# The third and fourth unit's weight scale within the first product, and VectorE work held behind a layer output's maximum

## The chip, the cores and the metric

The kernel runs on one core of a Trainium2 chip. TensorE (PE) multiplies, VectorE (DVE), ScalarE (ACT) and GpSimd (POOL) do the elementwise work, and SyncE (SP) issues DMAs. The metric is the device time of one execution in microseconds.

## The reference

Attention over 4 batches, 8 heads, 576 positions and 64 columns, whose softmax keeps only scores within `tau` = 0.02 of the row's maximum; then two feed-forward layers over the 2304 tokens, 512 to 2048 to 512 columns, all in f32:

```python
scores = scale * q @ k.T
scores = where(scores >= max(scores) - tau, scores, -1e9)
x = softmax(scores) @ v            # as (2304, 512)
h = x @ w_in;   x = (h * clip(h + 3, 0, 6) / 6) @ w_out      # layer 1
h = x @ w_in2;  out = (max(h, 0) ** 2) @ w_out2              # layer 2
```

## The kernel before, in words

**Precision.** Each f32 operand of a layer is split into an f16 high part and an f16 residue, scaled by a power of two, and a product is three f16 matmuls: high by high, residue by high, high by residue. The scales need maxima: of each group of weights, and of each layer's input.

**Blocks.** A batch of 576 tokens is one block. Layers and batches alternate: layer 1 of batch 0, layer 2 of batch 0, layer 1 of batch 1, and so on, eight blocks. A block takes 16 blocks of 128 hidden columns in four quarters. `hidden(f)` makes one of them: 24 matmuls into the PSUM tile `hp` (L685), then relu on ScalarE, `g` on VectorE (L690 or L693), the high part `gh` (L695, ScalarE) and the residue `gl` (L696, GpSimd). `output(qd)` multiplies a quarter with the output weights, four tiles `y` (L722), which VectorE adds to `ya` (L728) from the second quarter on.

**Borders.** Behind the last quarter of a layer 1, the block's output must be scaled for layer 2. For each of the four tiles there is an absolute maximum (L730); their maximum `gm` (L733) goes through a matmul `vm` (L119) which brings it to all partitions, then `mx` (L121), `ex` (L126) and the scale `sx` (L737). By it ScalarE (L386) and VectorE (L387) write the halves of the next layer's input, with which its first `hp` begins. The text calls the four passages from a layer 1 to its layer 2 the first to fourth border.

**Weights.** They come in units of 256 hidden columns, 1 MB each: 32 units, in the first two blocks alone (later blocks load the split weights back from DRAM). The order is `wseq`: two units of input weights, two more, two of output weights, and so on; so the third and fourth unit are input weights of the second quarter, and the fifth holds the first output weights. `group_scale` takes the scale of two units at once: an absolute maximum of each (L544, VectorE), `gm` (L546), again `vm` (L119), `mx` (L121), `sp` (L126, L550) and a few numbers of 128x1. `w_next` makes the halves: ScalarE scales (L611), VectorE shifts and merges bits (L614 and L615 for the first four units; for the others ScalarE's L619 and VectorE's merge L620), ScalarE writes the high part (L622), GpSimd the residue (L623), and SyncE stores both. There are 4 load buffers; a unit's buffer is free behind its merge.

**Order.** The program is written as generators: each step of a block asks `tick` for the weights that are due (`EARLY` gives the step at which the third to eighth unit are due, `LEAD` that of all later ones), and after each step the main loop hands out a share of the attention of the next batch (`attn_to`): scores, the softmax in two parts, the transposes of the probabilities by DMA, and five tiles later the product with v. A scheduler then sets the order in which each engine issues. `tc.issue_after(i)` gives it an edge: what is traced inside it on the engine of `i` is issued behind `i`. The tiles `s`, `hp` and `y` share three PSUM buffers; `vm`, the transposes and attention's product share two others.

## Time and profile before

| | |
|---|---|
| median of 3 runs | 1097.5 us (1095.11 to 1100.58) |
| profiled execution, its time | 1097.44 us |
| its span, first to last instruction | 1095.7 us |
| mean granted TensorE clock | 0.967 |
| TensorE busy | 1014.6 us (93%) |
| ScalarE busy | 654.4 us (60%) |
| VectorE busy | 642.9 us (59%) |
| GpSimd busy | 502.0 us (46%) |

Busy time is that of instructions that compute, weight loads aside; an engine that waits in its queue is idle. Of the 81 us in which TensorE isn't busy, most lies in the first 400 us, where attention of the first batches and the making of the weights go on beside the layers. A row's bracket tells how long the engine stood idle before it, and what released it.

### The profile page before, as it was taken

Reading aid. Unit: us, or ns where it says so; the run is one execution under the profiler, and the core shown is the slowest. Engines: PE = TensorE matmul, PEld = TensorE weight load, DVE = VectorE, ACT = ScalarE, POOL = GpSimd, SP = SyncE. Lnnn points to the kernel's source line nnn. Section 1 sums busy time; section 2 is a strip of 40 time slices with the busy share of each in tenths; the row PEclk is TensorE's granted clock in tenths of the full one; section 3 lists DMA queues with packets and bytes.
Section 4 is the critical chain, followed back from the end, with each engine's and each line's share of the span. In section 5 each row is a group of like instructions: output and inputs, shape, how many; then the busy total and the mean of one; then the engine's idle time right before and its main releaser. Section 6 shows DMA issues by size and latency. Waiting matters only on the chain.

```text
span 1095.7 us, 23283 instructions
## 1 busy us (share of the span) xinstructions
PE 1014.6 (93%) x9248; PEld 819.2 (75%) x9248; DVE 642.9 (59%) x1344; ACT 654.4 (60%) x1128; POOL 502.0 (46%) x629
## 2 busy tenths in 40 slices
PE   6877698897987999999999999999999999998998
PEld 4655476676776888888788888888788887776776
DVE  6885789889778875455855554555834231233122
ACT  5896798877887875655675555655654243313222
POOL 5886656755656754344355334443444222212111
PEclk9999799898988999999999999999999999999999
DMA  9999689896877686656565555555464342222211
GB/s 271 186 181 234 197 313 289 253 215 175 198 190 213 144 200 168 146 119 150 127 139 125 141 143 140 132 130 133 94 139 116 105 121 83 92 77 78 78 39 44
DMA packets 258748, 167.58 MB, mean 153 GB/s; under 512 B 215888, under 2 KB 228176, under 8 KB 258640
## 3 DMA queue, kind: packets, MB, share of 16 engines
q1 hardware_dynamic: 257072, 165.71, 60.3%
q8 instruction: 72, 1.18, 0.4%
q10 hardware_dynamic: 1568, 0.39, 0.2%
q14 instruction: 36, 0.29, 0.1%
HBM read 98.57 MB, written 21.50 MB: 110 GB/s over the span
## 4 chain that ended last, share of the span: by engine, by line
PE 72%; DVE 13%; DMA 7%; ACT 5%; issue 2%; POOL 1%; ACTq 0%; POOLq 0%; DVEq 0%
PE hp L685 30%; PE y L722 30%; PE s L295 4%; PE o L350 4%; DMA pt<-p 2%; DVE nm L301 2%; DVE wc L620 2%; DMA wd<-in_moe_w_out_dram 1%; DVE e L318 1%; DMA vraw<-in_v_dram 1%; PE s L291 1%; DVE ya L728 1%; PE tps L180 1%; DMA pt<-wpo 1%; DMA wd<-in_moe_w_in_dram 1%
## 5 line engine op out<-in xcount | busy, mean ns | idle before, releaser
L685 PE MATMUL hp<-x,wpi 128*128 128x288 f16 x3072 | 405.7, 291 | 13.8 <-ACT wpi L622 5.2
L685 PEld LDWEIGHTS <-wpi 128*128 128x128 f16 x3072 | 300.1, 99 | 94.7 <-ACT wpi L622 5.5
L722 PEld LDWEIGHTS <-wpo 128*128 128x128 f16 x3072 | 297.5, 99 | 92.7 <-DVE e L318 7.9
L722 PE MATMUL y<-gh,wpo 128*128 128x288 f16 x2048 | 338.7, 288 | 15.9 <-DVE e L318 7.5
L696 POOL TENSOR_TENSOR gl<-g,gh 128x576 f16<-128x576 f32 x128 | 168.6, 1318 | 299.6 <-ACT gh L695 298.9
L722 PE MATMUL y<-gl,wpo 128*128 128x288 f16 x1024 | 209.2, 288 | 0.0
L301 DVE TENSOR_REDUCE nm<-s 128x1 f32<-128x576 f32 x144 | 107.6, 750 | 58.7 <-PE s L295 55.3
L728 DVE SCALAR_TENSOR_TENSOR ya<-y,yq,ya 128x576 f32<-128x576 f32 (+1 forms) x97 | 77.9, 809 | 97.5 <-PE y L722 97.3
L326 POOL TENSOR_TENSOR p<-e,p 128x512 f16<-128x512 f32 x108 | 127.2, 1178 | 0.0
L695 ACT ACTIVATE gh<-g 128x576 f16<-128x576 f32 x128 | 86.9, 680 | 56.0 <-DVE g L693 27.9
L318 DVE SCALAR_TENSOR_TENSOR e<-s,thr,e 128x576 f32<-128x576 f32 x108 | 87.9, 814 | 38.9 <-ACT e L311 38.0
L324 ACT ACTIVATE p<-e 128x576 f16<-128x576 f32 x108 | 73.5, 681 | 51.3 <-DVE e L318 41.1
L350 PE MATMUL o<-v,pt 128*128 128x64 f16 (+1 forms) x2016 | 90.5, 200 | 12.2 <-ACT os L357 4.0
L350 PEld LDWEIGHTS <-pt 128*128 128x128 f16 x2016 | 80.6, 101 | 24.1 <-issue 9.3
L295 PE MATMUL s<-k_st,q_st 128*128 128x288 f32 x480 | 94.5, 320 | 0.6 <-DVE g L690 0.3
L693 DVE TENSOR_TENSOR g<-g,hp 128x576 f32<-128x576 f32 x64 | 48.0, 750 | 64.6 <-ACT g L692 64.4
L690 DVE SCALAR_TENSOR_TENSOR g<-g,r_w,hp 128x576 f32<-128x576 f32 x64 | 51.9, 810 | 57.8 <-ACT g L689 57.7
L689 ACT ACTIVATE g<-hp,r_h,aq 128x576 f32<-128x576 f32 x64 | 52.9, 829 | 53.7 <-PE hp L685 52.9
L692 ACT ACTIVATE g<-hp,r_w 128x576 f32<-128x576 f32 x64 | 47.1, 736 | 57.1 <-PE hp L685 55.9
L311 ACT ACTIVATE e<-s,nm 128x576 f32<-128x576 f32 x108 | 78.5, 727 | 0.4
L325 POOL TENSOR_TENSOR p<-e,p 128x64 f16<-128x64 f32 x108 | 35.2, 326 | 95.0 <-issue 59.2
L333 POOL TENSOR_SCALAR sm<-sm,vsc 128x2 f32<-128x2 f32 (+1 forms) x80 | 23.0, 287 | 112.7 <-DVE e L318 99.7
(127 smaller groups left out, 1138.5 us busy)
## 6 DMA issues: line engine op xcount, KB each, us to landing
wpi<-scr SPq DMA_DIRECT2D x48, 512.0 KB, 3.7
wpo<-scr SPq DMA_DIRECT2D x48, 512.0 KB, 4.1
wd<-in_moe_w_in_dram SPq DMA_DIRECT2D x16, 1024.0 KB, 7.2
wd<-in_moe_w_out_dram SPq DMA_DIRECT2D x16, 1024.0 KB, 6.9
scr<-wpi SPq DMA_DIRECT2D x16, 512.0 KB, 6.9
scr<-wpo SPq DMA_DIRECT2D x16, 512.0 KB, 5.0
kraw<-in_k_dram SPq DMA_DIRECT2D x16, 256.0 KB, 4.3
vraw<-in_v_dram SPq DMA_DIRECT2D x16, 256.0 KB, 3.2
```

Of the source, the lines that this page charges most:

```text
L295: nc.tensor.matmul(s[:, half, 0:HALF], lhsT=u.qs[sl][:, cs], rhs=u.ks[sl][:, kk, c], start=i == 0, stop=i == len(ops) - 1)
L301: nc.vector.tensor_reduce(out=j.nm, in_=j.s, axis=AX.XY, op=ALU.min)
L311: nc.scalar.activation(out=j.e, in_=j.s, func=AF.Exp, bias=j.nm, scale=-1.0)
L318: nc.vector.scalar_tensor_tensor(out=j.e, in0=j.s, scalar=j.thr, in1=j.e, op0=ALU.is_le, op1=ALU.mult, accum_out=u.sm[:, col:col + 1])
L324: nc.scalar.activation(out=p16[:, 0:S], in_=e, func=AF.Copy)
L326: nc.gpsimd.tensor_tensor(out=p16[:, S + TAIL:], in0=e[:, 0:NT * P], in1=p16[:, 0:NT * P], op=ALU.subtract)
L350: nc.tensor.matmul(o[:, n * w:n * w + w], lhsT=j.pt[:, c, :], rhs=vv[:, hs, vc, :], start=i == 0, stop=i == len(ops) - 1)
L685: last_hp[0] = nc.tensor.matmul(hp[:, a, 0:HALF], lhsT=wsl(tag, "i", f, w, c), rhs=x[c][:, a * HALF:(a + 1) * HALF], start=i == 0, stop=i ...
L695: nc.scalar.activation(out=gh, in_=gf, func=AF.Copy)
L696: nc.gpsimd.tensor_tensor(out=gl, in0=gf, in1=gh, op=ALU.subtract)
L722: nc.tensor.matmul(a[:, k_, 0:HALF], lhsT=wsl(tag, "o", f, w, e), rhs=g[f][:, k_ * HALF:(k_ + 1) * HALF], start=i == 0, stop=i == len(ops) ...
L728: nc.vector.scalar_tensor_tensor(out=y, in0=av_, scalar=yq, in1=y, op0=ALU.mult, op1=ALU.add)
```

## The change

There are three edits. The third and fourth unit's scale (`group_scale`) was called where the third unit was made, in an edge behind the last matmul of the step before (`last_hp`); now it is called within the first `hp`, behind its third chunk of input columns of four. `EARLY` makes the third to eighth unit due one or two steps sooner. And `border` remembers the instruction of the layer 1 output's `gm`; from there to the fourth step of layer 2, weights and attention are traced in an edge behind it, so that their VectorE instructions are issued behind `gm`.

```diff
@@ -26,7 +26,7 @@
 FIRST_LD = 34
 FIRST_ATT = 15
 PRE = 6
-EARLY = {2: 3, 3: 3, 4: 4, 5: 5, 6: 6, 7: 8}
+EARLY = {2: 1, 3: 1, 4: 2, 5: 3, 6: 5, 7: 7}
 SPLIT = 34
 FIRST_DVE = 4
 N_G, N_PT = 3, 7
@@ -572,8 +572,6 @@
                 nc.vector.tensor_scalar(out=e_y[L][:, c], in0=a_w[L][:, c], scalar1=e_w[L][:, c], scalar2=eo, op0=ALU.mult, op1=ALU.mult)
         return sp
 
-    last_hp = [None]
-
     def norm_scale(q):
 
         n = NQ // UC
@@ -602,9 +600,6 @@
             return
         while n_ld[0] <= k:
             w_load()
-        if k == len(FIRST_W):
-            with tc.issue_after(last_hp[0].ins):
-                group_scale(k)
         sp = group_scale(k)
         d = w_raw.pop(k)
         c = t = wt.tile([P, UW], F32, name="wc", bufs=3)
@@ -637,12 +632,18 @@
         while n_sp[0] <= k:
             w_next()
 
+    border = [None]
+
+    def behind():
+        return tc.issue_after(border[0].ins) if border[0] is not None else nullcontext()
+
     def tick(step):
         while n_sp[0] < len(wseq):
             k = n_sp[0]
             if EARLY.get(k, UC * k - LEAD) > step:
                 break
-            w_next()
+            with behind():
+                w_next()
 
     def wsl(tag, kind, f, part, j):
         w = w_hl[wuse[(tag, kind, f // UC)]]
@@ -682,8 +683,11 @@
             for c in range(NC):
                 for w, x in ((0, xh), (1, xh), (0, xl)):
                     for a in range(2):
-                        last_hp[0] = nc.tensor.matmul(hp[:, a, 0:HALF], lhsT=wsl(tag, "i", f, w, c), rhs=x[c][:, a * HALF:(a + 1) * HALF], start=i == 0, stop=i == 3 * NC - 1)
+                        mm = nc.tensor.matmul(hp[:, a, 0:HALF], lhsT=wsl(tag, "i", f, w, c), rhs=x[c][:, a * HALF:(a + 1) * HALF], start=i == 0, stop=i == 3 * NC - 1)
                     i += 1
+                if gstep[0] == 1 and c == NC - 2:
+                    with tc.issue_after(mm.ins):
+                        group_scale(n_sp[0])
             g = me.tile([P, 2, HALF], F32, name="g", bufs=N_G)
             if layer == 1:
                 nc.scalar.activation(out=g, in_=hv, func=AF.Relu, bias=r_h[:, q:q + 1], scale=aq[q])
@@ -730,9 +734,10 @@
                     nc.vector.tensor_reduce(out=y4[:, e:e + 1], in_=ya[:, e, :], axis=AX.X, op=ALU.max, apply_absolute_value=True)
                     if e == NC - 1:
                         am = st.tile([P, 1], F32, name="gm", bufs=2)
-                        nc.vector.tensor_reduce(out=am, in_=y4, axis=AX.X, op=ALU.max)
+                        gm = nc.vector.tensor_reduce(out=am, in_=y4, axis=AX.X, op=ALU.max)
                         s2 = st.tile([P, 1], F32, name="sx", bufs=2)
                         xsc["e"] = st.tile([P, 1], F32, name="ex", bufs=2)
+                        border[0] = gm
                         unit_of(xsc["e"], all_max(am, ident_s))
                         nc.vector.reciprocal(out=s2, in_=xsc["e"])
                         split_scaled([ya[:, c, :] for c in range(NC)], s2)
@@ -823,7 +828,10 @@
 
         for g, _ in enumerate(moe(tag, layer, b, xs)):
             if nxt is not None:
-                attn_to(min(nxt + LAG, start + math.ceil(todo * (g + 1) / ng)))
+                with behind():
+                    attn_to(min(nxt + LAG, start + math.ceil(todo * (g + 1) / ng)))
+            if layer == 2 and g == 3:
+                border[0] = None
 
 
 # ---- launch: one core; inputs and outputs as the reference has them ----
```

VectorE in the first product, from the last part of x on. `x` is the first layer's input, `k_st` keys of attention, the first `mx` to `r_h` belong to the scale of the weights, `wc` to the weights themselves. Before:

```order
L379 SCALAR_TENSOR_TENSOR x_1581<-xT,sx,x_1581 128x256
L220 TENSOR_TENSOR k_st_94<-tps,k_st_94 64x256
L220 TENSOR_TENSOR k_st_96<-tps,k_st_96 64x256
L121 TENSOR_REDUCE mx<-vm 128x1
L690 SCALAR_TENSOR_TENSOR g<-g,r_w_106,hp 128x576
L121 TENSOR_REDUCE mx<-vm 128x1
L126 TENSOR_SCALAR sp<-mx 128x1
L556 TENSOR_SCALAR e_w_102<-mx 128x1
L556 TENSOR_SCALAR a_w_104<-mx 128x1
L690 SCALAR_TENSOR_TENSOR g<-g,r_w_106,hp 128x576
L126 TENSOR_SCALAR sp<-mx 128x1
L550 RECIPROCAL sp<-sp 128x1
```

And now, from the same instruction on:

```order
L379 SCALAR_TENSOR_TENSOR x_1581<-xT,sx,x_1581 128x256
L121 TENSOR_REDUCE mx<-vm 128x1
L126 TENSOR_SCALAR sp<-mx 128x1
L556 TENSOR_SCALAR e_w_102<-mx 128x1
L556 TENSOR_SCALAR a_w_104<-mx 128x1
L550 RECIPROCAL sp<-sp 128x1
L563 RECIPROCAL rw<-a_w_104 128x1
L564 TENSOR_SCALAR r_w_106<-rw,e_w_102 128x1
L565 TENSOR_SCALAR r_h<-rw,e_w_102 128x1
L677 TENSOR_SCALAR aq_1888<-e_w_102,r_w_106 128x1
L678 TENSOR_TENSOR aq<-aq_1888,ex 128x1
L121 TENSOR_REDUCE mx<-vm 128x1
```

The scale of the third and fourth unit has moved ahead of the first `g`, and so have the numbers that follow from it and the next `mx`, that of the first output weights.

VectorE at the first border, from the maximum `gm` to the scale `sx`. `nm`, `e`, `sm` and `os` are attention's softmax, `am` and `vsc` the scale of v, `q_st` queries; `wc` and `g_4139` are weights. Before:

```order
L733 TENSOR_REDUCE gm<-y_3258 128x1
L546 TENSOR_REDUCE gm<-g_3794 128x1
L591 RECIPROCAL r_w_107<-mx 128x1
L592 TENSOR_SCALAR a_w_105<-mx,e_w_103 128x1
L318 SCALAR_TENSOR_TENSOR e,sm<-s,thr,e 128x576
L230 SCALAR_TENSOR_TENSOR q_st_90<-tps,qs,q_st_90 64x64
L334 RECIPROCAL sm<-sm 128x1
L712 MEMSET y_11125 128x1
L121 TENSOR_REDUCE mx<-vm 128x1
L126 TENSOR_SCALAR ex<-mx 128x1
L737 RECIPROCAL sx<-ex 128x1
```

And now, from `gm` on:

```order
L737 TENSOR_REDUCE gm<-y_3258 128x1
L589 RECIPROCAL r_w_107<-mx 128x1
L590 TENSOR_SCALAR a_w_105<-mx,e_w_103 128x1
L301 TENSOR_REDUCE nm<-s 128x1
L318 SCALAR_TENSOR_TENSOR e,sm<-s,thr,e 128x576
L243 TENSOR_REDUCE am<-vraw 128x1
L301 TENSOR_REDUCE nm<-s 128x1
L615 SCALAR_TENSOR_TENSOR wc<-wc,wd 128x1024
L546 TENSOR_REDUCE gm<-g_3794 128x1
L243 TENSOR_REDUCE am<-vraw 128x1
L716 MEMSET y_11125 128x1
L230 SCALAR_TENSOR_TENSOR q_st_90<-tps,qs,q_st_90 64x64
```

...and from there to `sx`, with nothing left out between:

```order
L121 TENSOR_REDUCE mx<-vm 128x1
L318 SCALAR_TENSOR_TENSOR e,sm<-s,thr,e 128x576
L544 TENSOR_REDUCE g_4139<-wd 128x1
L334 RECIPROCAL sm<-sm 128x2
L318 SCALAR_TENSOR_TENSOR e,sm<-s,thr,e 128x576
L126 TENSOR_SCALAR ex<-mx 128x1
L230 SCALAR_TENSOR_TENSOR q_st_92<-tps,qs,q_st_92 64x256
L361 TENSOR_TENSOR os<-o,sm 128x2x64
L334 RECIPROCAL sm<-sm 128x1
L742 RECIPROCAL sx<-ex 128x1
```

Nine instructions stood between `gm` and `sx`, one of them of 128x576; now there are twenty, and nine of these are of 128x576 or more.

VectorE at the second border, from `gm` to `sx`. Before:

```order
L733 TENSOR_REDUCE gm<-y_7556 128x1
L251 TENSOR_SCALAR vsc<-vsc 128x1
L318 SCALAR_TENSOR_TENSOR e,sm<-s,thr,e 128x576
L712 MEMSET y_13828 128x1
L252 RECIPROCAL vsc<-vsc 128x1
L318 SCALAR_TENSOR_TENSOR e,sm<-s,thr,e 128x576
L121 TENSOR_REDUCE mx<-vm 128x1
L253 TENSOR_SCALAR vsc<-vsc 128x1
L361 TENSOR_TENSOR os<-o,sm 128x2x64
L126 TENSOR_SCALAR ex<-mx 128x1
L737 RECIPROCAL sx<-ex 128x1
```

And now, where `gm`, one `nm`, one `e` and `vsc` stand ahead of these rows:

```order
L301 TENSOR_REDUCE nm<-s 128x1
L716 MEMSET y_13828 128x1
L121 TENSOR_REDUCE mx<-vm 128x1
L361 TENSOR_TENSOR os<-o,sm 128x2x64
L252 RECIPROCAL vsc<-vsc 128x1
L318 SCALAR_TENSOR_TENSOR e,sm<-s,thr,e 128x576
L334 RECIPROCAL sm<-sm 128x1
L301 TENSOR_REDUCE nm<-s 128x1
L126 TENSOR_SCALAR ex<-mx 128x1
L253 TENSOR_SCALAR vsc<-vsc 128x1
L361 TENSOR_TENSOR os<-o,sm 128x2x64
L742 RECIPROCAL sx<-ex 128x1
```

Fourteen instructions stand between `gm` and `sx` in place of nine, three `nm`, two `e` and two `os` among them.

## Rows read from the trace of the kernel before

**Rows 1.** Windows (A:B, length in us): each engine's busy us, clock, DMA, GB/s.

```profile
160.00:170.00 10.00, 6.96 (x43) 5.15 (x42) 9.94 (x22) 9.93 (x15) 6.14 (x7) 0.84 0.81 245
190.00:200.00 10.00, 7.96 (x44) 5.45 (x45) 9.61 (x25) 9.83 (x15) 3.53 (x6) 0.66 0.66 117
450.00:500.00 50.00, 50.00 (x491) 41.22 (x489) 28.46 (x58) 28.93 (x54) 22.90 (x29) 1.00 0.62 144
530.00:547.00 17.00, 14.56 (x167) 12.78 (x167) 15.79 (x46) 11.52 (x23) 6.21 (x9) 0.90 0.49 116
```

**Rows 2.** Timeline of TensorE, first stage: start us, us, instruction, [idle before <-releaser].

```profile
123.21 0.66 PE L685 MATMUL hp<-x,wpi 128*128 128x288 f16 x2 [5.17 <-ACT wpi L622]
...
128.35 1.14 PE L722 MATMUL y<-gh,wpo 128*128 128x288 f16 x4 [4.48 <-ACT wpo L622]
```

**Rows 3.** Timeline of VectorE, same stage, same columns.

```profile
110.06 0.48 DVE L379 SCALAR_TENSOR_TENSOR x<-xT,sx,x 128x256 f16<-128x256 f32 x1 [0.64 <-ACT x L378]
...
113.73 0.29 DVE L121 TENSOR_REDUCE mx<-vm 128x1 f32<-128x128 f32 x1 [1.77 <-PE vm L119]
...
118.00 1.42 DVE L614 TENSOR_SCALAR wc<-wc 128x1024 int32<-128x1024 int32 x1
...
122.92 1.23 DVE L615 SCALAR_TENSOR_TENSOR wc<-wd,wc 128x1024 int32<-128x1024 int32 x1
124.06 3.14 DVE L620 SCALAR_TENSOR_TENSOR wc<-wc,wd 128x1024 int32<-128x1024 int32 x1
```

**Rows 4.** Timeline of all engines at the last border of two layers.

```profile
989.95 0.16 DVE L733 TENSOR_REDUCE gm<-y 128x1 f32<-128x5 f32 x1
...
992.22 1.02 PE L685 MATMUL hp<-x,wpi 128*128 128x288 f16 x6 [1.57 <-ACT x L386]
```

**Rows 5.** Timeline of VectorE at the first border.

```profile
252.06 0.81 DVE L728 SCALAR_TENSOR_TENSOR ya<-y,yq,ya 128x576 f32<-128x576 f32 x1
...
258.72 0.15 DVE L733 TENSOR_REDUCE gm<-y 128x1 f32<-128x5 f32 x1
...
260.79 0.16 DVE L737 RECIPROCAL sx<-ex 128x1 f32<-128x1 f32 x1
```

**Rows 6.** Timeline at the second border, VectorE and TensorE.

```profile
534.03 0.82 DVE L728 SCALAR_TENSOR_TENSOR ya<-y,yq,ya 128x576 f32<-128x576 f32 x1 [0.17 <-PE y L722]
...
537.68 0.15 DVE L733 TENSOR_REDUCE gm<-y 128x1 f32<-128x5 f32 x1
537.97 0.46 PE L119 MATMUL vm<-ident_s,gm 128*128 128x128 f32 x2 [1.94 <-DVE vsc L251]
...
539.98 0.16 DVE L737 RECIPROCAL sx<-ex 128x1 f32<-128x1 f32 x1
...
542.47 0.65 PE L685 MATMUL hp<-x,wpi 128*128 128x288 f16 x4
```

**Rows 7.** Timeline of ScalarE, first stage.

```profile
116.73 2.33 ACT L611 ACTIVATE wc<-wd,sp 128x1024 f32<-128x1024 f32 x2
...
127.24 1.06 ACT L622 ACTIVATE wpo<-wc 128x1024 f16<-128x1024 f32 x1 [2.00 <-DVE wc L620]
```

**Rows 8.** Line 620: ns shortest/median/longest, first and last start us, form.

```profile
L620 DVE SCALAR_TENSOR_TENSOR wc<-wc,wd x28: 1206/1220/3172, 124.1 to 377.7; 128x1024 int32<-128x1024 int32 x28
```

**Rows 9.** Lines of VectorE by form: busy us, mean ns | idle before, releasers.

```profile
L301 DVE TENSOR_REDUCE nm<-s 128x1 f32<-128x576 f32 x144 | 107.6, 750 | 58.7 <-PE s L295 55.3 <-PE s L291 2.7
L318 DVE SCALAR_TENSOR_TENSOR e<-s,thr,e 128x576 f32<-128x576 f32 x108 | 87.9, 814 | 38.9 <-ACT e L311 38.0
...
L544 DVE TENSOR_REDUCE g<-wd 128x1 f32<-128x1024 f32 x32 | 38.9, 1216 | 5.7 <-DMA wd<-in_moe_w_in_dram 4.4 <-DMA wd<-in_moe_w_out_dram 1.1
...
L243 DVE TENSOR_REDUCE am<-vraw 128x1 f32<-128x640 f32 x16 | 13.1, 816 | 11.8 <-DMA vraw<-in_v_dram 11.7
```

**Rows 10.** Timeline of TensorE: two products of one block of hidden columns.

```profile
192.84 5.40 PE L685 MATMUL hp<-x,wpi 128*128 128x288 f16 x24 [0.15 <-DVE e L318]
...
547.26 3.10 PE L685 MATMUL hp<-x,wpi 128*128 128x288 f16 x24 [0.51 <-DVE e L318]
```

More of the change, by code (lines that the diff above doesn't have):

```diff
@@ L2 @@
 from collections import deque
-from contextlib import ExitStack
+from contextlib import ExitStack, nullcontext
 import concourse.bass as bass
```

## The prediction, made before the result was known

> **What bounds the kernel now.** I read the stages first [rows 1]: from about 400 us on TensorE is busy without a gap (450 to 500: 50.00 of 50.00, clock 1.00). What can be won lies before that, while weights are still being made (160 to 170: VectorE busy 9.94 of 10 us and TensorE 6.96), and at the four borders of two layers (530 to 547: 14.56 of 17 us, clock 0.90).
>
> Then TensorE's waits in the first stage. It stood 5.17 us until 123.21 for the first weights of the third unit, and 4.48 us until 128.35 for the first weights of the fifth [rows 2]. Followed back on VectorE [rows 3], these start from the maximum `mx` of the third and fourth unit's scale at 113.73, after 1.77 us of waiting for TensorE's `vm`: that stands behind 18 matmuls of the first product in TensorE's queue. From `mx` it goes to the first weight arithmetic (L614, 118.00).
>
> Last the borders. At the last one nothing else wants VectorE: from `gm` at 989.95 to the next layer's first product at 992.22 are 2.27 us [rows 4]. At the first, VectorE starts the last `ya` at 252.06, `gm` only at 258.72 and the scale `sx` at 260.79 [rows 5]; at the second the same three are at 534.03, 537.68 and 539.98, the next product at 542.47 [rows 6]. So attention's work on VectorE stands in the way there, before `gm` more than behind it.
>
> **The first product.** The new order puts the first `vm` right behind the transposes of x, ahead of the 18 matmuls. `mx` then follows the last L379 (110.06 plus 0.48, [rows 3]): 110.55, which is 3.2 us earlier. The rest of the head by the same rows: `sp` 0.7 us later; ScalarE's two L611 from 111.25 (2.33 us both, [rows 7], half of it the first); the second scale's `mx`, now ahead of the arithmetic, at about 113.2, since its `vm` stands behind 14 of the 18 matmuls; the shift (1.42) and the merge (1.23) of the first unit end at 115.8. Behind a second shift and two `g` the second merge ends at 120.1. Before, the first shift began at 118.00, so that its merge ended at 120.7, and the second merge ended at 124.15. That frees two load buffers 4 to 5 us earlier, and the loads behind them can be reduced by L544 as much earlier.
>
> This is paid for on TensorE: the three `g` stand behind the scale and the shifts, the first at 117.3 instead of right behind `mx` at 114.0; the product of the fourth block of hidden columns needs the PSUM tile which that frees, so it starts 3.3 us later. The gap is where the 5.17 us of waiting were. The fifth follows without stopping, and `y` starts when ScalarE has the first half of the fifth unit's weights, which was L622 at 127.24 [rows 7] and by the new queue (one relu group, two `gh` and two L611 ahead) is at about 124.2: 3.0 us earlier. Behind the first two `y` matmuls the queue now holds the next `vm`, which waits for the second L544; that costs what it gains up to about 130, still before the point at which `y` runs through now.
>
> So the lead is 3.0 to 5.0 us at its source. Its lower bound is zero, or a loss of up to 1.9 by the stretched merge below; the upper one 5.0. From 160 VectorE is nearly full [rows 1], and a lead in a full queue is kept. I take 3.2, from the row nearest to it (`mx`). The earlier turns in EARLY change no instruction's count; from the ninth unit on the turn is as before, and the 512 KB writes and 1 MB loads are moved only with the merges that free them.
>
> One price can go with it. The merge L620 takes 1.22 us in the median, but 3.14 at 124.06 [rows 3], and 3.172 at most [rows 8]: a `wpi` residue ran on GpSimd beside it. The Trainium skill (SBUF — State Buffer, section SBUF: two separate sides) says that a VectorE instruction with two SBUF inputs and a GpSimd instruction that reads SBUF exclude each other for their whole length; the trace agrees (3.14 against 1.22). By that rule, merges moved closer to the residues would cost up to 1.9 us each, which speaks against this change. By the row the first merge was free before and the third was stretched; one more stretched merge makes the sum 1097.5, none leaves it.
>
> **The borders.** The edge holds back on VectorE all attention and weight work traced behind `gm`. The new order shows the gain ahead of `gm`, and shows where the work went.
>
> First border: from `ya` to `gm` there now stand `mx`, one maximum, `q_st` and little else, 2.4 us instead of 6.7. But between `gm` and `sx` there are now two `nm` (0.750), three `e` (0.814), two `am` (0.816), a merge (1.22) and an L544 (1.216) [rows 8, 9]: 8.0, with the small ones about 9.3 instead of 2.1. `ya` to `sx` becomes 11.7 instead of 8.7. One `e` and one `am` no longer stand ahead of `ya`, which brings it 1.6 earlier. Net: 1.4 us later. Bounds: 3.0 later (if `ya` waited for TensorE anyway) and 4.3 earlier (if what stands behind `gm` were hidden by the wait for `vm`).
>
> Second and third border (same order): `gm` comes right behind the maximum and `vsc`, at 535.7 instead of 537.68. Then `nm`, `e`, `nm` (2.3) put `mx` at 538.0; and `os`, `e`, another `nm`, `os` (2.1) stand between `mx` and `sx`: 540.3 instead of 539.98. ScalarE then still has one exponential, the threshold and the copy of v to do, so that the product stays within 0.3 us of its 542.47. I take zero for each, between 1 us lost and 3.5 won. Queued behind the held work are the probabilities and their transposes on SP; the product of attention comes five tiles later, which hides a delay of 3.4 us. Fourth border: no attention is left, the order is the same, zero.
>
> **The sum.** 3.2 earlier, 1.4 given back: 1.8 us. The profiled execution took 1097.4 us (span 1095.7), close to the median of 1097.5; 1097.4 - 1.8 = 1095.6.
>
> **Rivals.** (a) The borders open. If `ex` and `sx` are reached at once, as at the last border (2.27 us from `gm` to the product, [rows 4]), the second and third lose what TensorE idles there (17.00 - 14.56 = 2.4 us, [rows 1]) and what the clock of 0.90 costs there (14.56 x 0.10 = 1.5): 2 x 3.9 = 7.8. With the lead, 1097.4 - 3.2 - 7.8 = 1086.4. For it: `gm` is certainly earlier. Against it: `e` and `nm` stand between `mx` and `ex` in VectorE's in-order queue, and they need no late input.
>
> (b) Slower: the held work delays `sx`, TensorE has nothing else, and the next layer's product starts at the lower clock. TensorE waited 1.94 us at the second border before `vm` [rows 6], then had attention matmuls; in the new order these are done earlier and the wait comes right ahead of the product. 24 matmuls of a product took 5.40 us at 192.84, where the granted clock of the stretch was 0.66, so largely at 1.2 GHz, and 3.10 at 547.26 [rows 1, 10]. At two borders that is 2 x 2.3, with the first border's 3.0 and no lead left: 1097.4 + 4.6 + 3.0 = 1105.0. It decides where `sx` is more than 1 us later than now. Against it: only 1.5 us of new waiting right there.
>
> (c) The change doesn't reach the end: the lead is used up by 200 us, since VectorE and the loads set the pace there, and only the first border's loss stays: 1097.4 + 1.4 = 1098.8. For it: 9.94 of 10 us busy. Against it: a full engine keeps a lead.
>
> **How the numbers follow.** Forecast 0.48 (own range 1092 to 1100), (a) 0.20, (b) 0.17, (c) 0.15. Half a per cent, 5.5 us, is what a measurement of this kernel can tell from none: below 1092.0 and above 1103.0. Faster: nearly all of (a), 0.19, and 0.09 of the forecast's lower end, since every order behind 130 us is changed too: 0.28. Slower: most of (b), 0.14, and 0.05 of the others: 0.19. Same: 0.53. The range, 1086 to 1104, takes in (a) and most of (b)'s way.
>
> **What would show it.** Right: `mx` of the third unit near 110.6, the two waits of 5.17 and 4.48 gone or under 2 in sum, `y` running before 131; at the second border `gm` near 1.7 us behind the start of the last `ya`, but `sx` still 6 us behind it, and the product within 0.5 us of its old distance; at the first border `ya` to `sx` over 10 us. Wrong: `sx` within 2 us of `gm` at the second border (then a), the product there at the lower clock (then b), or weights of 200 us no earlier than now (then c).

## The result, and the profile after

The change made the kernel slower: 1106.8 us in the median of 9 runs (1104.7 to 1110.2) against 1099.1 (1095.1 to 1102.5) of the kernel before on the same chip, a ratio of 1.0073 [1.0054, 1.0092]. 1095.6 was forecast, with 1086 to 1104 as the range. The profiled execution took 1106.1 us, span 1104.3. Three single executions of 1502 to 3622 us (one each of e2, e3 and the kernel before) are left out of every median and ratio.

A view that makes the place of the loss plain is the start of VectorE's `g`, the ReLU product of a block of hidden columns: 16 instructions per layer and block of tokens, 128 in all. Each line below is one profiled execution, so that two or three us are chance; the last column is timed. "2nd border" is what the stretch from the 48th to the 54th `g` has over the kernel before (59.08 us), "3rd border" the same from the 80th to the 86th (57.93). The first border lies between the 16th and the 33rd. The fourth differs by no more than 1.3 us in any of the experiments, and in the changed kernel by 0.04.

```
                       start of g (us)          2nd     3rd     ratio to before
                       1st    16th    33rd    border  border    [95% interval]
before                114.1   235.6   420.3                     
after                 117.9   234.2   421.8    +3.6    +3.5     1.0073 [1.0054, 1.0092]
e1 product alone      120.8   241.1   425.1     0.0    +0.8     1.0013 [0.9990, 1.0037]
e8 the same again     118.5   242.2   426.4     0.0    +0.8     1.0015 [0.9990, 1.0040]
e2 edges alone        114.2   233.9   418.1    +3.4    +3.4     1.0071 [1.0043, 1.0098]
e3 edge for weights   119.1   241.8   427.0     0.0    +0.8     1.0030 [1.0010, 1.0051]
e4 softmax free       116.4   236.6   420.7    +2.4    +2.3     1.0048 [1.0023, 1.0072]
e5 behind the scale   115.6   230.9   417.3    +7.0    +4.3     1.0110 [1.0087, 1.0134]
e6 e5, bubble 6       119.2   239.7   429.3    +1.3    +1.0     1.0056 [1.0034, 1.0078]
e7 e6 without product 114.6   235.3   426.6    +1.3    +1.0     1.0102 [1.0073, 1.0130]
e9 place alone        117.1   226.6   414.5    +0.1    +0.2     0.9932 [0.9910, 0.9955]
e10 turns alone       114.3   232.3   420.0    +1.5    +1.8     1.0002 [0.9983, 1.0021]
e13 place and edges   116.9   229.5   420.6    +2.5    +2.4     1.0050 [1.0030, 1.0071]
e14 place, half turns 116.2   231.2   417.2     0.0     0.0     0.9984 [0.9967, 1.0001]
e15 place, other half 116.3   228.8   416.7     0.0    +1.1     1.0004 [0.9988, 1.0019]
```

The changed kernel lost 3.6 and 3.5 us at the second and third border, where zero was forecast, and its lead at the 16th `g` (1.4 us) was a lag of 1.5 at the 33rd. From the third border on the distance of 8.7 us is constant.

The stages first, as in [rows 1] (same columns). The window at the border is put where it lies now, and its inside is cut into three:

```profile
160.00:170.00 10.00, 7.04 (x47) 5.03 (x45) 9.12 (x17) 9.86 (x16) 7.39 (x6) 0.90 0.73 186
190.00:200.00 10.00, 8.61 (x75) 6.87 (x74) 9.90 (x23) 9.93 (x15) 6.37 (x10) 1.00 0.97 186
450.00:500.00 50.00, 50.00 (x489) 41.24 (x489) 28.87 (x58) 29.61 (x55) 24.04 (x30) 1.00 0.68 153
535.00:552.00 17.00, 12.78 (x125) 10.46 (x124) 14.46 (x46) 11.17 (x23) 7.77 (x12) 0.80 0.48 124
...
539.50:543.50 4.00, 1.07 (x29) 0.88 (x28) 3.97 (x22) 3.09 (x8) 3.11 (x5) 1.00 0.31 59
543.50:547.50 4.00, 3.09 (x21) 2.76 (x22) 4.00 (x10) 4.00 (x8) 0.58 (x1) 0.50 0.48 92
547.50:551.50 4.00, 4.00 (x23) 2.88 (x23) 2.04 (x6) 2.15 (x6) 3.82 (x6) 0.65 0.33 94
```

450 to 500 is as full as it was. At the border TensorE is busy for 12.78 of 17 us at a clock of 0.80, where [rows 1] have 14.56 at 0.90: first a hole (1.07 of 4 us), then work at half the clock (0.50, that is 1.2 GHz instead of 2.4), then at 0.65 on the mean of the two levels.

TensorE at the second border, to be laid beside [rows 6]:

```profile
537.49 0.46 PE L119 MATMUL vm<-ident_s,gm 128*128 128x128 f32 x2 [0.34 <-DVE gm L737]
537.79 0.98 PE L350 MATMUL o<-v,pt 128*128 128x64 f16 x28
...
539.74 0.98 PE L350 MATMUL o<-v,pt 128*128 128x64 f16 x28
...
544.41 1.67 PE L350 MATMUL o<-v,pt 128*128 128x128 f16 x14 [3.69 <-DMA pt<-p]
545.88 0.63 PE L180 MATMUL tps<-ident,kraw 128*128 128x128 f32 x2
546.30 1.17 PE L686 MATMUL hp<-x,wpi 128*128 128x288 f16 x4
```

The wait for `vm` (1.94 us in [rows 6]) has shrunk to 0.34, as meant. Then a new one of 3.69 us ends with the transposed probabilities `pt`; 14 matmuls of attention stand ahead of the next layer's product in TensorE's in-order queue, and hold it up until 546.30. VectorE in the same place:

```profile
535.48 0.82 DVE L732 SCALAR_TENSOR_TENSOR ya<-y,yq,ya 128x576 f32<-128x576 f32 x1 [1.92 <-PE y L726]
...
537.20 0.15 DVE L737 TENSOR_REDUCE gm<-y 128x1 f32<-128x5 f32 x1
...
537.93 0.81 DVE L318 SCALAR_TENSOR_TENSOR e<-s,thr,e 128x576 f32<-128x576 f32 x1
...
539.40 0.29 DVE L121 TENSOR_REDUCE mx<-vm 128x1 f32<-128x128 f32 x1
...
541.63 0.16 DVE L742 RECIPROCAL sx<-ex 128x1 f32<-128x1 f32 x1
```

`gm` comes 1.72 us behind the start of the last `ya` (3.65 in [rows 6]), but `sx` 6.15 behind it (5.95): the gain ahead of `gm` went behind it, as forecast. The product, however, starts 10.8 us behind `ya` in place of 8.4, although ScalarE has begun on x in time (L386 at 542.83, 7.35 behind `ya`; before, 7.47). What was late is the softmax product `e` at 537.93. In the kernel before it stood ahead of the last `ya`, and the 14 matmuls, the last of 42 in the second row, ran without a wait:

```profile
533.03 0.82 DVE L318 SCALAR_TENSOR_TENSOR e<-s,thr,e 128x576 f32<-128x576 f32 x1 [0.93 <-ACT e L311]
...
539.68 2.95 PE L350 MATMUL o<-v,pt 128*128 128x64 f16 x42 [0.24 <-DVE vsc L253]
```

ScalarE and GpSimd make p of `e`, and SyncE then issues the transposes. SyncE before, and after:

```profile
536.17 7.91 SPq L328 DMA_TRANSPOSE pt<-p  x3
```

```profile
541.13 3.06 SPq L328 DMA_TRANSPOSE pt<-p  x2
```

From the issue at 541.13 to the matmuls at 544.41 are 3.3 us. At the third border the row is the same: 14 matmuls `o` at 790.06 behind 3.68 us of waiting for `pt`.

The first stage, TensorE, beside [rows 2]:

```profile
112.64 0.46 PE L119 MATMUL vm<-ident_m,gm 128*128 128x128 f32 x2 [0.30 <-DVE x L379]
112.93 1.88 PE L686 MATMUL hp<-x,wpi 128*128 128x288 f16 x14
...
118.79 3.36 PE L686 MATMUL hp<-x,wpi 128*128 128x288 f16 x26 [3.05 <-DVE g L694]
...
122.76 2.87 PE L686 MATMUL hp<-x,wpi 128*128 128x288 f16 x22 [0.61 <-POOL wpi L618]
...
127.22 0.42 PE L726 MATMUL y<-gh,wpo 128*128 128x288 f16 x2 [1.59 <-ACT wpo L617]
130.03 0.49 PE L119 MATMUL vm<-ident_m,gm 128*128 128x128 f32 x2 [2.39 <-DVE gm L546]
```

And VectorE, beside [rows 3] (L609, L610 and L615 are the old L614, L615 and L620):

```profile
112.88 0.48 DVE L379 SCALAR_TENSOR_TENSOR x<-xT,sx,x 128x256 f16<-128x256 f32 x1 [0.39 <-ACT x L378]
113.28 0.28 DVE L121 TENSOR_REDUCE mx<-vm 128x1 f32<-128x128 f32 x1
...
115.28 0.68 DVE L609 TENSOR_SCALAR wc<-wc 128x1024 int32<-128x1024 int32 x1
...
117.92 0.81 DVE L694 SCALAR_TENSOR_TENSOR g<-g,r_w,hp 128x576 f32<-128x576 f32 x1
...
121.68 2.10 DVE L615 SCALAR_TENSOR_TENSOR wc<-wc,wd 128x1024 int32<-128x1024 int32 x1
```

x itself came later in this execution (its last part at 112.88, before at 110.06, with the same order ahead of it). Counted from there the head did what it was to do: `mx` 0.4 us behind the last part of x instead of 3.7, the two waits of 5.17 and 4.48 us now 3.05, 0.61 and 1.59, and the first `y` at 14.3 us behind x instead of 18.3.

Two things make that less than it looks. TensorE's clock helped: behind x it was at 1.00 here and at 0.50 in the kernel before (108.8 to 112.2). With the old order and the clock at 1.00, as in e7 below, the first `y` is 17.3 us behind x, so that the order brings 2.9 of the 4.0 us. And only two matmuls of `y` come that early. Behind them the next `vm` waits 2.39 us, as the prediction said, and the 24th matmul of `y` is 24.3 us behind x, where the kernel before has 25.9 and e7 24.5.

### The profile page after: what moved, and what is told of

The parts are those of the page before. It is cut to its first block, busy times and chain, and to the rows that moved or that the text cites. A ratio compares the mean times of both kernels' runs of the same rounds, so it can differ in the third digit from the quotient of the medians.

```text
span 1104.3 us, 23281 instructions
## 1 busy us (share of the span) xinstructions
PE 1019.3 (92%) x9248; PEld 821.5 (74%) x9248; DVE 642.2 (58%) x1344; ACT 654.8 (59%) x1128; POOL 502.1 (45%) x629
## 3 DMA queue, kind: packets, MB, share of 16 engines
q8 instruction: 72, 1.18, 0.4%
## 4 chain that ended last, share of the span: by engine, by line
PE 66%; DVE 11%; DMA 9%; ACT 9%; issue 2%; POOL 2%; SPq 0%; ACTq 0%; POOLq 0%; DVEq 0%
PE y L726 29%; PE hp L686 27%; PE s L295 4%; PE o L350 3%; DMA wd<-in_moe_w_out_dram 2%; DVE wc L615 2%; DMA pt<-p 2%; DMA wd<-in_moe_w_in_dram 2%; DMA pt<-wpo 2%; ACT wc L606 1%; DVE e L318 1%; DVE nm L301 1%; DVE g L544 1%; PE s L291 1%; DMA vraw<-in_v_dram 1%
## 5 line engine op out<-in xcount | busy, mean ns | idle before, releaser
L686 PE MATMUL hp<-x,wpi 128*128 128x288 f16 x3072 | 402.0, 289 | 10.8 <-DVE g L694 3.0
L696 ACT ACTIVATE g<-hp,r_w 128x576 f32<-128x576 f32 x64 | 47.1, 736 | 63.2 <-PE hp L686 62.9
```

Of the source, the lines that this page charges most:

```text
L686: mm = nc.tensor.matmul(hp[:, a, 0:HALF], lhsT=wsl(tag, "i", f, w, c), rhs=x[c][:, a * HALF:(a + 1) * HALF], start=i == 0, stop=i == 3 * N ...
```

## The experiments: the borders

**The edges alone.** The kernel before, with `border` and `behind()` and nothing else.

```diff
+            with behind():
+                w_next()
...
+                with behind():
+                    attn_to(min(nxt + LAG, start + math.ceil(todo * (g + 1) / ng)))
```

> The kernel before with the edges behind the maximum and nothing else. Theory A: 1097.4 + 4.9 + 3.6 + 3.6 = 1109.5, with the wait for a transposed probability tile of 3.7 us on TensorE at the second and third border. Rival B: 1097.4 + 7.2 = 1104.6, nothing lost at the first border.

Measured: 1106.1 us, 1.0071 [1.0043, 1.0098]. The two borders take 3.4 us more each, and TensorE's row at the second is that of the changed kernel:

```profile
540.87 1.68 PE L350 MATMUL o<-v,pt 128*128 128x128 f16 x14 [3.68 <-DMA pt<-p]
542.34 0.64 PE L180 MATMUL tps<-ident,kraw 128*128 128x128 f32 x2
542.77 1.17 PE L691 MATMUL hp<-x,wpi 128*128 128x288 f16 x4
```

So the edges alone make the whole loss. At the first border this kernel loses nothing that shows in the stretch from the 16th to the 33rd `g` (184.2 us against 184.6): the border itself, from the 16th to the 17th, takes 39.3 us against 35.0, and the 4.3 us are made up behind it. The profiled execution is the shortest of this kernel (1102.1 us), so that 3 of the 7.7 us between the medians do not show in it.

**Which edge.** The first product with the edge kept for weights only (attention free), and the first product without any edge, twice:

```diff
-                with behind():
-                    attn_to(min(nxt + LAG, start + math.ceil(todo * (g + 1) / ng)))
+                attn_to(min(nxt + LAG, start + math.ceil(todo * (g + 1) / ng)))
```

> The changed kernel with the edge for weight work alone; attention is free. No weight is made after 400 us. Theory A (attention's held softmax is what costs): the second and third border cost nothing, the first at most part of its 4.9: 1094 to 1097. Rival B: 1098.9. If the held weights are what costs at the first border: 1099.

> The changed kernel without any edge behind the maximum; the scale within the first product and the earlier turns stay. Theory A (the edges cost 4.9, 3.6 and 3.6 us at the first three borders, the first product gives 3.4): all three losses go, 1097.4 - 3.4 = 1094.0; the second border's product starts 4.8 us behind the last ya's start... as in the kernel before (8.4 us from ya to the product). Rival B (the loss ahead of 420 us is the earlier turns' doing, and only the second and third border are the edges'): 1097.4 + 1.5 = 1098.9, with the g instructions of 420 us 1.5 us late.

> The changed kernel without any edge, once more, for its trace: its 12 times fell into two groups, 1093.6 to 1098.5 and 1102.3 to 1104.3. If the two groups are the granted clock of the first product (TensorE idle ahead of it for 2.7 us, and 14 matmuls in 3.14 us in the slow trace, in 1.88 us in the trace of the kernel with the edge behind sx), a trace of the fast group shows 1.88 there and the y of the first layer some 4 us sooner behind the last part of x; if not, the difference arises later.

Measured: 1102.1, 1100.4 and 1100.3 us. In all three the second border costs nothing and the third 0.8 us: it is attention's edge that costs there. The product alone gains nothing in the time; the 12 runs of e1 fall into two groups, 1093.6 to 1098.5 and 1102.3 to 1104.3 us, but e8 has three of its 8 between them (1099.7 to 1100.3), so that two groups are not shown. Both profiled executions lie at the upper end (1104.1 and 1103.9 us), for which the lines e1 and e8 stand; a trace from the lower end, which e8 was to bring, is missing. That no gain came was open at this point (next section).

**The late transposes.** The changed kernel, with the second half of the softmax, which makes `e` and p, free of the edge:

```diff
-                with behind():
-                    attn_to(min(nxt + LAG, start + math.ceil(todo * (g + 1) / ng)))
+                attn_to(min(nxt + LAG, start + math.ceil(todo * (g + 1) / ng)))
...
-                scores(j)
-                soft1(j)
+                with behind():
+                    scores(j)
+                    soft1(j)
```

> The changed kernel, with attention's second part of the softmax (the threshold product e and what makes the probabilities and their transposes) traced outside the edge; scores, maxima and the rest stay behind gm. Theory A (late transposes: at the second and third border the 14 matmuls of attention that stand ahead of the next product in TensorE's queue wait 3.7 us for a transpose, whose e the edge moved from 533.0 to 537.9): the wait goes, and the two borders lose under 1 us each in place of 3.6: about 1100. Rival D (the product is late because sx is, or because the maxima are held): each still loses 3 or more, 1106.

Measured: 1104.2 us, 1.0048 [1.0023, 1.0072]; +2.4 and +2.3 us at the two borders. TensorE at the second:

```profile
540.66 0.95 PE L350 MATMUL o<-v,pt 128*128 128x128 f16 x14 [0.82 <-DVE e L318]
...
543.71 0.65 PE L689 MATMUL hp<-x,wpi 128*128 128x288 f16 x4 [0.73 <-ACT x L386]
...
548.42 1.17 PE L689 MATMUL hp<-x,wpi 128*128 128x288 f16 x8 [1.58 <-DVE x L387]
```

The wait of 3.7 us for the transposes is gone, but only 1.2 us of 3.6 come back, which neither theory had. What is late next is x: ScalarE has p and `os` ahead of it in its queue, and then VectorE's low half L387 holds the product for 1.58 us more.

**The edge further back.** Everything held until `sx`, not `gm`, so that nothing of attention stands between the two:

```diff
-                        border[0] = gm
...
-                        nc.vector.reciprocal(out=s2, in_=xsc["e"])
+                        border[0] = nc.vector.reciprocal(out=s2, in_=xsc["e"])
```

> The changed kernel with the edge behind the scale sx instead of the maximum gm, so that nothing held stands between the two. Theory A: what cost was that the held work stands between gm and sx and that the product of attention stands ahead of the next layer's product in TensorE's queue; here the new order has the first product ahead of the 14 matmuls that wait for the last transposes, so sx comes within 2 us of gm, and the product of the second and third border starts 2 us earlier than in the kernel before: 1097.4 - 3.4 - 2 x 2 = 1090, and the first border no worse than before. Rival C (the transposes are late wherever the edge is, and TensorE lacks work): TensorE stops as long behind the first products, 1104 or more.

Measured: 1110.8 us, 1.0110 [1.0087, 1.0134]. VectorE and then TensorE at the second border:

```profile
533.11 0.15 DVE L737 TENSOR_REDUCE gm<-y 128x1 f32<-128x5 f32 x1
...
534.42 0.17 DVE L741 RECIPROCAL sx<-ex 128x1 f32<-128x1 f32 x1
...
542.02 0.80 DVE L318 SCALAR_TENSOR_TENSOR e<-s,thr,e 128x576 f32<-128x576 f32 x1
```

```profile
542.88 5.92 PE L686 MATMUL hp<-x,wpi 128*128 128x288 f16 x24 [6.06 <-DVE e L318]
```

`sx` comes 1.3 us behind `gm`, as at the last border, and is worth nothing: the product waits 6.06 us for the PSUM tile that attention's scores hold until `e` has read them. That tile can be given back by letting fewer scores run ahead at the border (`BUBBLE` 8 to 6), with the first product and without:

```diff
-BUBBLE = 8
+BUBBLE = 6
```

> The kernel with the edge behind the scale sx, with BUBBLE 6 in place of 8, so that one tile of attention less is handed out between the last output step and the next layer: the order has two tiles of scores ahead of the product instead of three, and the third PSUM tile is free for it. Theory A' (behind sx, what stopped TensorE for 6.06 us was the PSUM tile that the third tile of scores held until its e): the product of the second and third border starts within 6 us of the last ya's start (8.4 in the kernel before, 11.5 behind sx with BUBBLE 8), the two borders gain about 3 us each over the kernel before, 1094. Rival C (TensorE only idles elsewhere, since its attention work is held): they gain nothing or lose, 1100 or more.

> The kernel before with nothing but the edge behind sx and BUBBLE 6. Theory A': as in the run with both, about 3 us gained at the second and third border each, 1098.4 - 6 = 1092 if the first border costs nothing. If the first product's edit were worth its 3.4 us to the end, this would be 3.4 slower than the run with both; if it is worth nothing (as 1100.4 of its own run says), the two agree or this is faster. Rival C: 1098 or more.

Measured: 1105.3 us, 1.0056 [1.0034, 1.0078], and 1108.3, 1.0102 [1.0073, 1.0130]. TensorE at the second border of the first of them:

```profile
548.15 0.65 PE L686 MATMUL hp<-x,wpi 128*128 128x288 f16 x4 [0.62 <-ACT x L386]
...
549.98 2.47 PE L686 MATMUL hp<-x,wpi 128*128 128x288 f16 x18 [1.18 <-DVE x L387]
...
553.45 0.41 PE L686 MATMUL hp<-x,wpi 128*128 128x288 f16 x2 [1.00 <-DVE x L387]
```

Here the product starts 4.65 us behind the last `ya` (543.50), against 8.4 before. It then stops for the low halves of x (1.18 and 1.00), and attention comes behind it: the border is still 1.3 us longer than before. In the second kernel the stretch with the first border took 191.3 us, 6.7 more than before, which is most of its loss. By the sign in the second text, the first product is worth 3.0 us here (1108.3 without it, 1105.3 with it; the two intervals just overlap), where alone it is worth nothing: its price depends on what stands behind it. None of the orders of VectorE's work that were run at the border beats the old one.

## The experiments: the first product

**Its two parts apart.** The first product changes two things: the place of the third and fourth unit's scale, and the turns in `EARLY`. The place with the old turns, and the new turns in the kernel before:

```diff
 e9, against the product alone
-EARLY = {2: 1, 3: 1, 4: 2, 5: 3, 6: 5, 7: 7}
+EARLY = {2: 3, 3: 3, 4: 4, 5: 5, 6: 6, 7: 8}
 e10, against the kernel before
-EARLY = {2: 3, 3: 3, 4: 4, 5: 5, 6: 6, 7: 8}
+EARLY = {2: 1, 3: 1, 4: 2, 5: 3, 6: 5, 7: 7}
```

> The changed kernel without any edge and with the old turns (EARLY as before): only the scale's place within the first product is new. Both runs of the whole first part gave 1100.3 where 3.4 us of gain were expected, 1095. Theory E (the place is worth its 3 us, the earlier turns, which put two shifts and two merges ahead of the first layer's g and its loads and stores ahead of attention's, give it back): 1095 to 1096. Theory F (the lead is lost wherever it comes from, as the making of the weights is paced elsewhere, by SyncE's queue and the clock): 1099 to 1101, as with the turns.

> The kernel before with the new turns alone; the scale behind the last matmul of its step, as before. Theory E: slower, 1101 or more. Theory F: 1098 to 1101.

Measured: the place alone takes 1091.5 us (1090.3 to 1094.4), 0.9932 [0.9910, 0.9955], faster than both kernels; the turns alone 1099.9, 1.0002. Together (the product alone, above) they make 1.0013. So the turns take back what the place brings, though alone they cost nothing: theory E is right on the place and wrong on the turns (1101 or more). The granted clock (the number before the last two) of the place alone and of the product alone, with the DMA share and GB/s behind it:

```profile
140.00:180.00 40.00, 36.95 (x290) 28.94 (x288) 34.30 (x74) 35.36 (x50) 22.09 (x23) 1.00 0.83 269
180.00:240.00 60.00, 52.69 (x497) 43.06 (x496) 51.64 (x101) 50.91 (x77) 41.72 (x41) 1.00 0.98 270
```

```profile
140.00:180.00 40.00, 37.04 (x282) 29.05 (x280) 34.19 (x69) 36.84 (x53) 25.17 (x22) 0.95 0.88 285
180.00:240.00 60.00, 51.27 (x475) 41.02 (x474) 48.63 (x99) 49.72 (x70) 36.40 (x37) 0.94 0.96 258
```

With the place alone TensorE runs the stretch from 140 to 240 at the full clock and does 787 matmuls in it, with the turns too 757. The executions are of 1092.9 and 1104.1 us, 11 apart where the medians are 9 apart.

In the trace of the product alone the lead is gone before the first tile of `y` is done. TensorE's clock, and then its rows:

```profile
109.70:113.70 4.00, 1.59 (x30) 1.20 (x30) 0.94 (x3) 1.60 (x6) 0.00 (x0) 1.00 0.56 56
113.70:117.10 3.40, 3.15 (x13) 2.20 (x14) 1.98 (x12) 2.09 (x3) 0.00 (x0) 0.50 0.00 0
```

```profile
114.51 3.14 PE L685 MATMUL hp<-x,wpi 128*128 128x288 f16 x14
...
135.10 0.80 PE L119 MATMUL vm<-ident_m,gm 128*128 128x128 f32 x2 [4.74 <-DVE gm L546]
```

After 4 us with 1.59 us of work the clock fell, ahead of the first instruction whose place is new (`vm` at 113.95), so it is not the lead that brought it there. The 14 matmuls ahead of the second scale took 3.14 us instead of 1.88, the maximum for the next `vm` came later, and that `vm` waits 4.74 us where the changed kernel waits 2.39. The 24th matmul of `y` is 27.3 us behind x, against 25.9 in the kernel before. In e3, e4, e6 and e8, whose order is the same up to there, the clock fell too (14 matmuls in 2.84 to 3.41 us), and the 24th comes at 26.8 to 27.6; in the changed kernel and in e5 it stayed at 1.00, and the 24th comes at 24.3 and 23.1. So in these seven executions the product with both parts has a lead there only where the clock behind x stayed full.

**Place and edges.** The changed kernel with the old `EARLY`.

> The changed kernel with the old turns: the scale's new place and the edges behind gm. If the edges' cost is their own (3.5 us at the second and third border each, none at the first, as in the run of the edges alone): 1091.5 + 7 = 1098.5. If it comes only together with the new turns: 1092.

Measured: 1104.3 us, 1.0050 [1.0030, 1.0071]. The 16th `g` is 6.2 us ahead of the kernel before, the 33rd level with it, and the second and third border take 2.5 and 2.4 us more. Against the place alone the edges cost some 13 us: 5 at these two borders, 1.2 at the fourth, and 6 are missing at the 33rd `g` (420.6 for 414.5), 3 of them at the 16th already, ahead of any instruction inside an edge. So the two parts do not add up.

**Which turns.** The product alone with new turns for the third and fourth unit only, and for the fifth to eighth only:

```diff
+EARLY = {2: 1, 3: 1, 4: 4, 5: 5, 6: 6, 7: 8}
...
+EARLY = {2: 3, 3: 3, 4: 2, 5: 3, 6: 5, 7: 7}
```

> No edge; the new place, and the new turns for the third and fourth unit alone (1 and 1; the others 4, 5, 6 and 8 as before). Theory G (what takes the lead back is the earlier turn of the fifth to eighth unit, whose loads and stores the order puts ahead of the next keys in SyncE's queue): 1092, as with the old turns. Theory H (it is the third and fourth unit's, with the second scale ahead of the first merge and the three g behind both shifts): 1100.

> No edge; the new place, and the new turns for the fifth to eighth unit alone (2, 3, 5 and 7; the third and fourth 3 and 3 as before). Theory G: 1100, and the keys (kraw) are issued on SyncE behind two loads of weights and two stores. Theory H: 1092.

Measured: 1096.9, 0.9984 [0.9967, 1.0001], and 1099.1, 1.0004 [0.9988, 1.0019]. Either half takes back most of the gain, which neither theory had. The profiled executions (1095.6 and 1096.5 us) are 1 to 3 us below these medians and show less of it. SyncE issues the loads of the next keys at 130.47 in the second, behind the loads of weights that the earlier turns bring, at 114.24 in the first and at 115.87 with the place alone. So late keys can be the way of the second half, but not of the first; with the turns alone, which cost nothing, they come at 136.67. Of the second half's loss 0.9 us lies at the third border, where no weight is made any more: an edit in the first block changes the scheduler's order there too (the turns alone lose 1.5, 1.8 and 0.9 us at the second to fourth border, without any edge).

**The queue of the stores.** SyncE's queue holds the stores of the finished weights among the loads. The product alone, and the kernel before, with these stores issued by GpSimd:

```diff
-        nc.sync.dma_start(out=dr, in_=w)
+        nc.gpsimd.dma_start(out=dr, in_=w)
```

> The changed kernel without any edge, with the stores of the split weights issued by GpSimd, behind the residue that they wait for, instead of by SyncE. Theory F' (the lead is lost in SyncE's in-order queue: in the changed kernel's trace the load of the 16th unit is issued at 169.1, 7.5 us behind that of the 15th, with a store and a transpose that waited in between, where before both went at 164.9): the loads no longer wait for residues, the 15th and 16th unit's maxima (L544) follow one another within 3 us again, and the first part keeps its 3 us: about 1095. Against it: GpSimd issues and its stores cost it time, so that both this and its control may be slower; what counts is the difference to the control.

> Control: the kernel before with the stores issued by GpSimd and nothing else. Theory F': within 3 us of 1098.6, and 3 us slower than the kernel with the first part and the same stores. If SyncE's queue doesn't matter, the two differ as the two without it, by 1.5 us the other way.

Measured: 1115.4, 1.0153 [1.0123, 1.0182], and 1114.6, 1.0141 [1.0117, 1.0164]. Both lose some 15 us, and the kernel with the first product stays the slower one, by 0.8 us. So the lead did not come back with the stores off SyncE; but a kernel that loses 15 us by the move may lose the lead in another way, so that this speaks against the stores and does not rule them out.

## Why the prediction was wrong

**Second and third border: zero taken, 3.6 and 3.5 measured.** The orders were read rightly (`gm` 1.7 us behind `ya`, `sx` 6 behind it, ScalarE on x in time). The step that failed is "the product of attention comes five tiles later, which hides a delay of 3.4 us". `e` came 4.9 us later in the trace (537.93 for 533.03; 3.5 of it against the last `ya`, which was 1.45 later itself), and the 14 matmuls that need its transposes stand right ahead of the product in TensorE's queue, not five tiles behind it. In the kernel before they stand there too, but their transpose was issued 5.0 us sooner (536.17 for 541.13). Now they waited 3.69 us, and the product then began at the lower clock. The edges alone show the same wait and the whole loss; with the transposes in time the wait is gone, and x is late instead. I followed the held work up to SyncE and did not look up which matmul in TensorE's queue takes its result.

**The first product: 3.2 us gained was taken, 1.4 lost [1.1 gained to 4.1 lost] measured.** At its source the step held for the first `y`, 4.0 us nearer to x, of which 1.0 is the clock; at the 24th `y` it is down to 1.6, and to 0.2 against e7, where the old order had the full clock too. Failed is "a full engine keeps a lead", together with "the earlier turns in EARLY change no instruction's count", costed at nothing. The place alone keeps its lead, and more than I gave it (7.5 us by its ratio); with the new turns nothing of it reaches the end. Which of the moved instructions takes it back is not settled: late keys fit one half of the turns, and SyncE's stores are made unlikely. The clock is a rival: with both parts there is no lead at the 24th `y` in the executions whose clock fell behind x. Only the place alone has it at 1.00 in both later stretches shown above (0.90 to 1.00 elsewhere), and there it may as well follow from the lead as bring it; no run moved the clock by itself.

**The first border: 1.4 us lost was taken.** `ya` to `sx` came out at 12.45 us (forecast 11.7, [rows 5] have 8.7), with the held work where the prediction had it (`gm` 2.3 behind `ya`). But most of what is over 8.7 is not the edge's: without any edge, `ya` to `sx` is 11.5 us with the place alone and 10.7 with the product alone, so that the edge adds 1 to 2 us there, not 3.0. With the edges alone it is 13.5, and yet the stretch loses nothing; with the place and the edges a lead of 6.2 us at the 16th `g` is gone at the 33rd, where the place alone loses 3.3 of 9.1. So its price depends on what is ahead, and how much of it is the border's own stays open.

**The stretched merge.** The price of up to 1.9 us did not come: the third merge took 2.10 us where [rows 3] have 3.14, and the longest of its line 3.04 where [rows 8] have 3.17. By the rule of the Trainium skill (SBUF — State Buffer, section SBUF: two separate sides), VectorE with two SBUF inputs shuts out a GpSimd instruction that reads SBUF and the other way; the trace agrees: the third merge began at 121.68 beside a residue on GpSimd (119.78 to 122.71) and ended 1.07 us behind it. Only the collisions cost no more than before: of 32 merges 10 took over 1.3 us (8 before), all of them together 6.5 us more than at 1.22 each (6.8 before).

**The rivals.** (b) was right in sign and, at 1105.0, near in size; what came late was the product of attention and not `sx`. (a) fell: even with `sx` 1.3 us behind `gm`, PSUM and the low halves of x come next. (c) has one thing right, a lead that is used up, but for the place with the new turns and not for the place. The sum by what was measured: edges alone +7.8 us, first product alone +1.4 with an interval that holds zero, against +8.0 for the change. Of the 7.8, 6.9 are seen at the second and third border.

## What to carry to other kernels

An instruction held back on one in-order queue is paid for where its result is taken: follow it through every engine to the consumer, and see what stands behind that consumer in its queue (3.69 us for a transpose, 6.06 for a PSUM tile), before the cost is put at nothing. In a window in which VectorE has no free time none of the four orders tried here gained: what was let past made something else late. Two parts that look like one edit are run apart: here the one alone was worth 0.7%, and the two together nothing. And a trace is one execution: where it lies among the times of its kernel, and at which clock, is read before it is laid beside another.

## What was not expected of the hardware

- The shift of 128x1024 int32 on VectorE took 0.68 us four times out of four in the changed kernel, and 0.68 to 1.77 in the one before (1.42 at 118.00, [rows 3]). The two slow ones began while GpSimd was making the residues `gl` (L696, 116.35 to 118.88 and 119.72 to 121.82); in the changed kernel the shifts of 115.28 and 117.32 were over when GpSimd began at 119.78:

```profile
L609 DVE TENSOR_SCALAR wc<-wc x4: 683/684/689, 83.1 to 117.3; 128x1024 int32<-128x1024 int32 x4
```

```profile
L614 DVE TENSOR_SCALAR wc<-wc x4: 681/1050/1768, 79.2 to 120.6; 128x1024 int32<-128x1024 int32 x4
```

- At the second border TensorE's clock fell to 0.50 within a wait of 3.69 us, and stood at 0.65 on the mean of the 4 us in which it then worked without a gap. The Trainium skill (TensorE: Matmul & The Clock Gate, Part 1: The HAM clock gate (the "warmup" mystery)) says that "the default state is throttled, and activity releases the throttle"; the trace agrees.
- 32 stores of 512 KB issued by GpSimd instead of SyncE cost 15 us in two kernels.
